# HGRN2 attention and a PReLU network on one core: the second layer by Strassen's seven products

## The chip, the core and the metric

The kernel runs on one NeuronCore of a Trainium2 chip. TensorE multiplies matrices into PSUM, VectorE and ScalarE work on tiles in SBUF and PSUM, GpSimd works on SBUF and issues transfers, and the sync engine issues transfers. The metric is the device time of one execution in microseconds, from the first to the last instruction on the core. Lower is better.

## What is computed

The first half is a gated linear recurrence over 768 time steps for 4 batches and 8 heads of dimension 48. Its output, rearranged to 3072 tokens of 384 numbers, goes through a two-layer network with a leaky activation whose slope is learned per column.

```python
f = 1 / (1 + exp(-f_logit))
for t in range(768):
    state = f[:, :, t, :, None] * state + einsum('bhd,bhe->bhde', k[:, :, t], v[:, :, t])
    y[:, :, t] = einsum('bhd,bhde->bhe', q[:, :, t], state)
x = y.transpose(0, 2, 1, 3).reshape(3072, 384)
h = x @ w_in                                     # 384 x 2048
g = maximum(h, 0) + alpha * minimum(h, 0)
out = g @ w_out                                  # 2048 x 384
```

All tensors are float32.

## The kernel before

Time is cut into chunks of C = 128, and a step handles one chunk of a pair of batches (U = 2), so a step has 256 tokens and there are 12 steps: `steps` runs over the six chunks, and within each over the two pairs. For each step there are four generators. Each does a piece of work up to a `yield`:

- `prepare` ("Q" for the step to come, "P" at the start) loads f, q, k, v, takes the sigmoid (L277), and builds the decayed forms of q and k on VectorE with some copies on ScalarE. It has six pieces. Lines L285 to L292 are in the first, the two scans L315 and L317 in the second, L319, L345 and the first L328 in the third, L366, L372 and further L328 in the fourth and fifth, the transpose L420 and the copies L415 in the sixth.
- `carry` ("O") has the matmuls `off` (L442) and `pd` (L482) and moves the recurrent state (`moved`, L492 and L496).
- `attend` ("S") has the matmuls `raw` (L518) and `qu` (L533) with masked copies on VectorE (L524, L539), the copies of `ad` into A on ScalarE (L561, eight of them in two pieces), the matmuls `py` (L572), and the copies and transfers that turn their result into xT, the network's input.
- `network` ("n") is the two-layer network of the step before.

The network has eight pieces for the first layer. Each multiplies two 128-column blocks of w_in with the 256 tokens of xT into one PSUM bank `ph` (L614); ScalarE takes relu(-h) (L620), and VectorE combines the two into the gate tile g (L623, two instructions). Four pieces for the second layer follow: the 16 row blocks of the gate against w_out, 128x384 a time, for the two batches of the step, 32 f32 matmuls in all (L639). Each f32 matmul is two records on TensorE in the profile. ScalarE copies the two results (L633), and the sync engine stores them. The gate is the stationary operand here and w_out is streamed.

PSUM has two pools: `psa`, two tiles of two banks that attention takes in turn, and `psn`, four single banks that `ph` and the second layer's results take in turn. A tile can be taken once the readers of the tile four takings earlier are done.

The order of the instructions on TensorE, VectorE and ScalarE is the order in which the generators are advanced. It is written out by hand as strings of letters, with a count where a piece is repeated: `first` has the strings of the opening rounds, `usual` that of all later ones. A generator that has no step left is passed over, so the last round has only "n".

```python
usual = "O n S n2 S n2 O n Q n Q2 n2 S3 n Q S n Q n Q"
```

At the start, the pieces "a", "w", "b", "v" bring w_in and w_out in: they are loaded as 64-bit words and turned to float32 with staging tiles, and the last part of w_out is added by transfers that GpSimd issues (L225).

Of the kernel before, what the change touches and what calls it, by code (L numbers as in the profile page):

```python
# [8 lines left out]
F32 = mybir.dt.float32  # L9
I16 = mybir.dt.int16  # L10
U16 = mybir.dt.uint16
BF16 = mybir.dt.bfloat16
# [3 lines left out]
ALU = mybir.AluOpType  # L16

C = 128
# [3 lines left out]
U = 2  # L22
# [3 lines left out]
WP = 768  # L26
AT_ONCE = 1
RAWS, TOPS, POWERS, LEADS = 4, 3, 1, 4
# [3 lines left out]
def kernel(  # L32
# [30 lines left out]
    nc = tc.nc  # L63
    B, NC, _, HP, _ = qT.shape
    DM = v.shape[-1]
    H = 2 * HP
    D = DM // H
    NF = alpha.shape[1]
    NK = DM // 128
    DF = NF * 128  # L70
    T = U * C
    W = U * HP * C
    GC = W // CH
    G = W // DB
    NJ = C // DB
# [11 lines left out]

    const = ctx.enter_context(tc.tile_pool(name="const", bufs=1))
    work = ctx.enter_context(tc.tile_pool(name="work", bufs=2))
    psa = ctx.enter_context(tc.tile_pool(name="psa", bufs=2, space=bass.MemoryType.PSUM))  # L90
    psn = ctx.enter_context(tc.tile_pool(name="psn", bufs=4, space=bass.MemoryType.PSUM))

# [3 lines left out]
    def bank(name):  # L96
        return psn.tile([128, 512], F32, tag="net", name=name)

    om = const.tile([128, NF], F32, tag="om", name="om")
    w_in_sb = const.tile([128, NK, DF], F32, tag="w_in", name="w_in_sb")  # L100
    w_out_sb = const.tile([128, NF, DM], F32, tag="w_out", name="w_out_sb")
    lvl = const.tile([128, 2, DB], F32, tag="lvl", name="lvl")
    nc.scalar.dma_start(out=lvl, in_=masks)
    nc.scalar.dma_start(out=om, in_=alpha)
# [58 lines left out]
    def load_weights(dst, src, name):  # L163

        rows_ = NK if dst is w_in_sb else 1
        pieces_ = dst.shape[1] * dst.shape[2] // WP
        if rows_ == 1:
            dst = dst.rearrange("p a n -> p (a n)").unsqueeze(1)
        width = WP // rows_
        words = src.rearrange("p (a n) -> p a n", a=rows_).bitcast(I16)  # L180
        at_once = AT_ONCE if rows_ > 1 else 0
        got = {}

        def of(n):
            return dst[:, :, n * width:(n + 1) * width]

        def by_row(t):
            return t.rearrange("p (a n) -> p a n", a=rows_)

        def upper(n):  # L190
            raw = work.tile([128, WP, 4], I16, tag="raw", name=f"{name}_raw{n}", bufs=RAWS)
            nc.sync.dma_start(out=raw.rearrange("p (a n) four -> p a (n four)", a=rows_)[:, :, 0:4 * width - 1],
                              in_=words[:, :, 4 * n * width + 1:4 * (n + 1) * width])

            top = raw[:, :, 2]
            pos = work.tile([128, WP], I16, tag="pos", name=f"{name}_pos{n}", bufs=TOPS)
            nc.scalar.activation(pos, top, AF.Relu, bias=bias[:, 0:1], scale=8.0)
            neg = work.tile([128, WP], I16, tag="wneg", name=f"{name}_neg{n}", bufs=TOPS)
            nc.scalar.activation(neg, top.bitcast(U16), AF.Relu, bias=bias[:, 1:2], scale=8.0)
            got[n] = raw, pos, neg  # L200

        def lead(n):
            raw, pos, neg = got[n]
            t = work.tile([128, WP], BF16, tag="lead", name=f"{name}_lead{n}", bufs=LEADS)
            nc.vector.tensor_tensor(t, pos.bitcast(BF16), neg.bitcast(BF16), ALU.subtract)
            got[n] = raw, t

        def power(n):
            raw, t = got[n]
            p = work.tile([128, WP], BF16, tag="power", name=f"{name}_power{n}", bufs=POWERS)  # L210
            nc.vector.tensor_scalar(p.bitcast(I16), t.bitcast(I16), -128, None, ALU.bitwise_and)
            got[n] = raw, t, p

        def rest(n):
            raw, t, p = got.pop(n)
            got[n] = t
            low = raw.bitcast(U32)[:, :, 0]
            nc.vector.scalar_tensor_tensor(of(n), by_row(low), 2.0 ** -36, by_row(p), ALU.mult, ALU.mult)

        def both(n):  # L220
            t = by_row(got.pop(n))
            if n < at_once:
                nc.vector.tensor_tensor(of(n), of(n), t, ALU.add)
            else:
                nc.gpsimd.dma_start(out=of(n), in_=t, accum_op=ALU.add)  # L225

        def uppers():
            for n in range(pieces_):
                upper(n)
                yield  # L230

        def rests():
            for n in range(pieces_ + 1):
                if n < pieces_:
                    lead(n)
                if n:
                    rest(n - 1)
                if n < pieces_:
                    power(n)
                if n:  # L240
                    both(n - 1)
                yield

        return uppers(), rests()
# [11 lines left out]
    def prepare(bp, c, x):  # L256
# [159 lines left out]
                               q3[rows(par)].rearrange("p (u h c) s t -> p u h c (s t)", h=HP, c=NC2)[:, :, :, cc, 0:CH])  # L416
        if c:

            kt = work.tile([128, 2 * WP], F32, tag="raw", name=f"kt_{i}", bufs=RAWS)
            nc.vector.transpose(kt[:, 0:W], ks.rearrange("p g s t -> p (g s t)"))  # L420
            ksn = x["ksn"] = work.tile([128, U, HP * 128], F32, tag="ksn", name=f"ksn_{i}", bufs=1)
            for a in range(4):
                n = min(32, D - 32 * (a % 2))
                for b in range(NJ):
                    nc.sync.dma_start(
                        out=ksn[32 * b:32 * (b + 1)].rearrange("p u (h x) -> p (u h) x", h=HP)[:, :, 32 * a:32 * a + n],
                        in_=kt[32 * a:32 * (a + 1), 0:W].rearrange("p (g b x) -> p g b x", b=NJ, x=32)[:, :, b, 0:n])
        yield

    def carry(bp, c, x):  # L430
# [175 lines left out]
    def network(bp, c, x):  # L606
        i = f"{bp}_{c}"
        xT = x["T"]
        gs = []
        for f in range(0, NF, 2):  # L610
            ph = bank(f"ph{f}_{i}")
            for kt in range(NK):
                for j in range(2):
                    nc.tensor.matmul(ph[:, j * T:(j + 1) * T], lhsT=w_in_sb[:, kt, (f + j) * 128:(f + j + 1) * 128],  # L614
                                     rhs=xT[:, kt], start=(kt == 0 and j == 0), stop=(kt == NK - 1 and j == 1),
                                     skip_group_check=True)

            neg = work.tile([128, 2, T], F32, tag="neg", name=f"neg{f}_{i}")
            phv = ph.rearrange("p (j t) -> p j t", j=2)
            nc.scalar.activation(neg, phv, AF.Relu, scale=-1.0)  # L620
            g = work.tile([128, 2, T], F32, tag="g", name=f"g{f}_{i}", bufs=8)
            for j in range(2):
                nc.vector.scalar_tensor_tensor(g[:, j], neg[:, j], om[:, f + j:f + j + 1], phv[:, j],  # L623
                                               ALU.mult, ALU.add)
            gs.append(g)
            yield

        po = [bank(f"po{u}_{i}") for u in range(U)]
        last = (bp, c) == steps[-1]

        def store(u):
            o = work.tile([128, DM], F32, tag="o", name=f"o{u}_{i}")
            nc.scalar.copy(o, po[u][:, 0:DM])  # L633
            t0 = ((U * bp + u) * NC + c) * C
            nc.sync.dma_start(out=out[t0:t0 + C], in_=o)

        for n, (f, u) in enumerate([(f, u) for u in range(U) for f in range(NF)] if last else
                                   [(f, u) for f in range(NF) for u in range(U)]):
            nc.tensor.matmul(po[u][:, 0:DM], lhsT=gs[f // 2][:, f % 2, u * C:(u + 1) * C], rhs=w_out_sb[:, f],  # L639
                             start=(f == 0), stop=(f == NF - 1))  # L640
            if last and (f, u) == (NF - 1, 0):
                store(0)
            if n % 8 == 7 and n != U * NF - 1:
                yield
        for u in range(1 if last else 0, U):
            store(u)
        yield

    steps = [(bp, c) for c in range(NC) for bp in range(B // U)]
    first = (
        "P2 a P w P a P a w O P w S a w S Q a O a w S2 Q w S Q S",
        "P a w a P w2 b n2 v O n b2 v S n v n P S b S v b n S v n b v Q b n b n v O v n v Q3 S2 n2 Q2",
        "O n2 S n2 S Q S2 n3 O n Q n Q2 n S2 n Q2 n",
        "n O n2 S n2 S Q n O Q n2 S Q n S n S Q2 S Q n2",
    )
    usual = "O n S n2 S n2 O n Q n Q2 n2 S3 n Q S n Q n Q"  # L660
    pieces = {key: part for keys, parts in (("aw", load_weights(w_in_sb, w_in, "w_in")),
                                            ("bv", load_weights(w_out_sb, w_out, "w_out")))
              for key, part in zip(keys, parts)}

    def begin(n):
        if n >= len(steps):
# [70 lines left out]
```

## Time and profile before

| | |
|---|---|
| time, median of 3 runs | 650.63 us (650.04 to 652.03) |
| span of the profiled execution | 649.8 us |
| TensorE matmuls (PE) busy | 608.4 us, 94% of the span |
| VectorE (DVE) busy | 423.8 us, 65% |
| ScalarE (ACT) busy | 255.0 us, 39% |
| GpSimd (POOL) busy | 67.7 us, 10% |
| first layer, L614 | 1152 records of 128x256 |
| second layer, L639 | 768 records of 128x384 |

PE means matmuls and PEld the loads of the stationary operand, which have their own row. A line such as `L639 PE MATMUL po<-w_out_sb,g 128*128 128x384 f32 x768` has the line in the kernel, the engine, what is written from what, the stationary shape, the moving shape and the number of instructions. In a wait such as `[1.01 <-ACT qd L280]`, the engine stood idle for 1.01 us before the instruction and ScalarE's instruction at line 280 ended that. An idle time matters only where it reaches the engine that sets the end.

### The profile page before, as it was taken

What the parts mean: (1) busy time and instruction counts of PE and PEld (TensorE: products, weight loads), DVE (VectorE), ACT (ScalarE), POOL (GpSimd) and SP (SyncE); (2) the same over time, 40 slices, a digit from 0 to 9 for tenths busy, and PEclk for the clock granted to TensorE, in tenths of its full rate; (3) what the DMA queues carried; (4) which work ended last, traced back from release to release, by engine and by line L of the source; (5) the groups of instructions that cost most, each with busy time, mean ns of one, the idle gap of its engine ahead of it and who ended that gap; (6) DMA issues with size and microseconds to landing.
All of it is one profiled execution on the core that took longest, in us unless ns stands there. A gap on an engine that the chain in (4) does not pass through costs nothing.

```text
span 649.8 us, 17589 instructions
## 1 busy us (share of the span) xinstructions
PE 608.4 (94%) x7580; PEld 451.3 (69%) x7580; DVE 423.8 (65%) x866; ACT 255.0 (39%) x466; POOL 67.7 (10%) x114
## 2 busy tenths in 40 slices
PE   0549799999999999999999999999999999999997
PEld 0447666866876876875875876876876786786874
DVE  6889788794595685686686687577577477450220
ACT  5676683432443161361360360461351351331210
POOL 9142221000000010000000000001001000000000
PEclk9998899999999999999999999999999999999999
DMA  7998985412223223313313313313313201101000
GB/s 256 274 251 224 270 223 133 100 47 61 45 80 74 73 56 72 72 41 86 73 35 90 74 34 90 75 34 90 65 44 88 49 30 35 42 1 25 24 1 24
DMA packets 73116, 56.22 MB, mean 87 GB/s; under 512 B 47408, under 2 KB 64944, under 8 KB 73040
## 3 DMA queue, kind: packets, MB, share of 16 engines
q0 software_dynamic: 10112, 27.53, 15.9%
q1 hardware_dynamic: 57536, 25.37, 15.6%
q10 hardware_dynamic: 5392, 2.21, 1.6%
q8 instruction: 60, 0.98, 0.6%
q14 instruction: 16, 0.13, 0.1%
HBM read 36.21 MB, written 4.72 MB: 63 GB/s over the span
## 4 chain that ended last, share of the span: by engine, by line
PE 91%; DVE 5%; issue 2%; ACT 1%; DMA 1%; DVEq 0%
PE ph L614 39%; PE po L639 38%; PE py L572 3%; PE raw L518 3%; PE qu L533 3%; PE pd L482 1%; PE off L442 1%; DMA f<-in_fT 1%; DVE ad L524 1%; PE pk L469 1%; DVE qd L285 0%; PE off L452 0%; DVE us L319 0%; DVE k L345 0%; ACT us L312 0%
## 5 line engine op out<-in xcount | busy, mean ns | idle before, releaser
L614 PE MATMUL ph<-xT,w_in_sb 128*128 128x256 f32 x1152 | 263.5, 386 | 3.9 <-issue 3.9
L639 PE MATMUL po<-w_out_sb,g 128*128 128x384 f32 x768 | 252.9, 488 | 0.0
L614 PEld LDWEIGHTS ph<-xT,w_in_sb 128*128 128x128 f32 x1152 | 217.6, 192 | 37.3 <-issue 7.5
L639 PEld LDWEIGHTS po<-w_out_sb,g 128*128 128x128 f32 x768 | 144.9, 190 | 96.8
L623 DVE SCALAR_TENSOR_TENSOR g<-neg,om,ph 128x256 f32<-128x256 f32 x192 | 83.2, 476 | 164.6 <-ACT neg L620 164.5
L620 ACT ACTIVATE neg<-ph 128x512 f32<-128x512 f32 x96 | 57.4, 600 | 169.1 <-PE ph L614 164.3
L633 ACT COPY o<-po 128x384 f32<-128x384 f32 x24 | 11.5, 478 | 145.5 <-PE po L639 145.5
L524 DVE COPY_PREDICATED ad<-mraw,raw 128x256 f32<-128x256 int32 (+1 forms) x96 | 42.3, 441 | 5.5 <-PE raw L518 3.0
L539 DVE COPY_PREDICATED ad<-mquad,qu 128x224 f32<-128x224 int32 (+6 forms) x140 | 41.9, 299 | 6.2
L561 ACT COPY A<-ad 32x256 f32<-32x256 f32 x96 | 38.4, 400 | 2.2 <-DVE ad L539 0.9
L328 DVE TENSOR_TENSOR us<-us,fs 128x768 f32<-128x768 f32 (+5 forms) x60 | 37.1, 618 | 0.3
L312 ACT COPY us<-qd 128x256 f32<-128x256 f32 x48 | 30.3, 668 | 9.9 <-DVE qd L285 9.8
L264 POOL DMA_DIRECT2D k<-in_kT x11 | 8.3, 759 | 233.7 <-PE raw L518 206.9
L285 DVE TENSOR_TENSOR qd<-qd,f 128x768 f32<-128x768 f32 (+2 forms) x36 | 27.1, 753 | 8.2 <-ACT qd L280 8.2
L572 PEld LDWEIGHTS py<-A,vs 128*64 128x64 f32 x768 | 25.0, 145 | 10.3 <-ACT A L561 8.1
L415 ACT COPY A<-q 48x512 f32<-48x512 f32 x44 | 27.1, 616 | 9.4 <-DVE f L410 4.5
L572 PE MATMUL py<-A,vs 128*64 128x64 f32 x768 | 26.9, 231 | 3.9 <-ACT A L561 3.9
L518 PE MATMUL raw<-qd,k 48*32 48x80 f32 x1536 | 23.7, 243 | 5.2 <-issue 3.9
L518 PEld LDWEIGHTS raw<-qd,k 48*32 48x32 f32 x1536 | 18.5, 109 | 13.6 <-issue 13.0
L442 PE MATMUL off<-q,kh 48*32 48x32 f32 x768 | 9.4, 199 | 18.4 <-DVE q L366 18.4
L581 ACT COPY y<-py 128x512 f32<-128x512 f32 x24 | 12.9, 589 | 34.2 <-PE py L572 34.1
L533 PE MATMUL qu<-us,k 48*32 48x112 f32 (+1 forms) x1536 | 25.7, 259 | 0.0
(85 smaller groups left out, 437.7 us busy)
## 6 DMA issues: line engine op xcount, KB each, us to landing
w_out_raw<-in_w_out SPq DMA_DIRECT2D x8, 767.8 KB, 6.4
w_in_raw<-in_w_in SPq DMA_DIRECT2D x8, 767.2 KB, 6.2
f<-in_fT POOLq DMA_DIRECT2D x11, 512.0 KB, 4.1
q<-in_qT POOLq DMA_DIRECT2D x11, 512.0 KB, 4.0
k<-in_kT POOLq DMA_DIRECT2D x11, 512.0 KB, 4.4
out<-o SPq DMA_DIRECT2D x24, 192.0 KB, 2.1
vs<-in_v POOLq DMA_DIRECT2D x22, 192.0 KB, 3.7
w_out_sb<-w_out_lead POOLq DMA_DIRECT2D x8, 384.0 KB, 6.3
```

The lines of the kernel that those rows point to most:

```text
L312: nc.scalar.copy(q4[:, :, :, r], qdv[r][:, :, :, 0])
L328: nc.vector.tensor_tensor(us[:, :, UO[m]:UO[m] + 4 * n].rearrange("p g (i r) -> p g i r", r=4), us[:, :, skip:skip + 4 * n].rearrange("p g ...
L518: nc.tensor.matmul(raw[DB * j:DB * (j + 1), par, hp * C:hp * C + QW], lhsT=k[r_, g * DB:(g + 1) * DB], rhs=qd[r_, g], start=True, stop=True)
L524: nc.vector.copy_predicated(adu[:, :, :, d:4], mraw[:, d, :, d:4].bitcast(I32).unsqueeze(1).broadcast_to((128, H, NB, n)), rv[:, :, QO[d]: ...
L533: nc.tensor.matmul(qu[DB * j:DB * (j + 1), par, hp * QS + 4:hp * QS + QL], lhsT=k4[r_, g * DB:(g + 1) * DB], rhs=us[r_, g, 4:QL], start=Tr ...
L539: nc.vector.copy_predicated(ad[:, u, :, :, 4 * m:DB], mquad[:, lo:lo + n].bitcast(I32).unsqueeze(1).unsqueeze(1).broadcast_to((128, 2, HP, ...
L561: nc.scalar.copy(A[s_, u, :, s_], ad[s_, u].rearrange("p r h t -> p (r h) t"))
L572: nc.tensor.matmul(py[64 * par:64 * par + 64, u, o:o + CH], lhsT=vs[bp][:, cc, u, hd * D:hd * D + 64], rhs=A[:, u, par * HP + hp, CH * cc: ...
L614: nc.tensor.matmul(ph[:, j * T:(j + 1) * T], lhsT=w_in_sb[:, kt, (f + j) * 128:(f + j + 1) * 128], rhs=xT[:, kt], start=(kt == 0 and j == ...
L620: nc.scalar.activation(neg, phv, AF.Relu, scale=-1.0)
L623: nc.vector.scalar_tensor_tensor(g[:, j], neg[:, j], om[:, f + j:f + j + 1], phv[:, j], ALU.mult, ALU.add)
L639: nc.tensor.matmul(po[u][:, 0:DM], lhsT=gs[f // 2][:, f % 2, u * C:(u + 1) * C], rhs=w_out_sb[:, f], start=(f == 0), stop=(f == NF - 1))
```

## The change

From the second step on, the second layer is computed as a product of 2 x 2 blocks. The tokens of the two batches are the two block rows of the gate, the two halves of the 2048 hidden columns its block columns, and w_out is cut into halves by rows and by columns. Winograd's form of Strassen's scheme needs seven products of half-size blocks (each eight matmuls of 128x192) where the plain form needs eight. In exchange it adds and subtracts blocks: four sums of gate blocks (S), four of w_out blocks (t1 to t4), and sums of the products.

- The gate becomes one tile that is kept for the whole kernel. In a changed step, the first layer's groups pair block f with block f + 8, so that both halves of the hidden columns come along together. After groups 4 and 8, VectorE makes the four gate sums for the four row blocks just finished (`sums`).
- The w_out sums are made once, on GpSimd, in the piece "W" (`halves_of_w_out`) of the second round, after the first step's network, which stays plain. t1 overwrites the block b12.
- The staging tiles of the weight loads move to a pool of their own, which is closed before the new tiles are allocated. The tile `kt` of L420, which shared a staging buffer, gets its own.
- Products one (a11 b11) and two (a22 t4) need no gate sum. Product one is copied by ScalarE (`kept`) and added on VectorE to product three; banks of products one and three go on accumulating products five and six. In all, six adds out of PSUM on VectorE and two copies on ScalarE replace the two copies of L633.
- The network has five pieces for the second layer in place of four, the last of them an add and a store alone; the order strings are extended, and in `usual` the third preparation piece moves behind the eighth first-layer group.

```diff
-        for f in range(0, NF, 2):
+        plain = (bp, c) == steps[0]
+        for f in range(NH):
             ph = bank(f"ph{f}_{i}")
+            tiles = (2 * f, 2 * f + 1) if plain else (f, f + NH)
...
-            g = work.tile([128, 2, T], F32, tag="g", name=f"g{f}_{i}", bufs=8)
-            for j in range(2):
-                nc.vector.scalar_tensor_tensor(g[:, j], neg[:, j], om[:, f + j:f + j + 1], phv[:, j],
+            for j, m in enumerate(tiles):
+                nc.vector.scalar_tensor_tensor(gate[:, m % NH, m // NH], neg[:, j], om[:, m:m + 1], phv[:, j],
                                                ALU.mult, ALU.add)
+            if not plain and f % 4 == 3:
+                sums(slice(f - 3, f + 1))
             yield
...
+        def product(to, of, by, more=False):
+            for f in range(NH):
+                nc.tensor.matmul(to[:, 0:DH], lhsT=of(f), rhs=by(f), start=(f == 0 and not more), stop=(f == NH - 1),
+                                 skip_group_check=True)
...
+        product(pa, a11, b11)
+        product(pb, a22, t4)
+        nc.scalar.copy(kept, pa[:, 0:DH])
+        yield
+        pc, pd = (bank(f"p{n}_{i}") for n in "cd")
+        product(pc, s2, t2)
+        product(pd, s1, t1)
+        nc.vector.tensor_tensor(u2, pc[:, 0:DH], kept, ALU.add)
+        yield
+        product(pa, a12, b21, more=True)
+        product(pc, s3, t3, more=True)
+        nc.vector.tensor_tensor(o0[:, DH:DM], pd[:, 0:DH], u2, ALU.add)
+        nc.scalar.copy(o0[:, 0:DH], pa[:, 0:DH])
+        yield
+        pe = bank(f"pe_{i}")
+        product(pe, s4, b22)
+        nc.vector.tensor_tensor(u3, pc[:, 0:DH], kept, ALU.add)
+        nc.vector.tensor_tensor(o1[:, 0:DH], pb[:, 0:DH], u3, ALU.add)
+        nc.vector.tensor_tensor(o1[:, DH:DM], pd[:, 0:DH], u3, ALU.add)
+        store(1, o1)
+        yield
+        nc.vector.tensor_tensor(o0[:, DH:DM], pe[:, 0:DH], o0[:, DH:DM], ALU.add)
+        store(0, o0)
+        yield
...
+        for to, x_, y_, op in ((s[:, 0, fs_], of(0, u1), of(1, u1), ALU.add),
+                               (s[:, 1, fs_], s[:, 0, fs_], of(0, u0), ALU.subtract),
+                               (s[:, 2, fs_], of(0, u0), of(0, u1), ALU.subtract),
+                               (s[:, 3, fs_], of(1, u0), s[:, 1, fs_], ALU.subtract)):
+            nc.vector.tensor_tensor(to, x_, y_, op)
...
+        for to, x_, y_ in ((late["t3"], b22, b12), (b12, b12, b11), (late["t2"], b22, b12), (late["t4"], b21, late["t2"])):
+            nc.gpsimd.tensor_tensor(to, x_, y_, ALU.subtract)
...
-    usual = "O n S n2 S n2 O n Q n Q2 n2 S3 n Q S n Q n Q"
+    usual = "O n S n2 S n2 O n Q n Q n Q n S3 n Q S n Q n Q n"
```

## Prediction

> **What bounds the kernel now.** I read the page first (busy shares, then the chain), then the chain in order of time for the period of a step, then the groups by shape for prices, then the timeline of one middle step, 308.6 to 358.1 us.
>
> ```profile
> PE 608.4 (94%) x7580; PEld 451.3 (69%) x7580; DVE 423.8 (65%) x866; ACT 255.0 (39%) x466; POOL 67.7 (10%) x114
> ...
> PE 91%; DVE 5%; issue 2%; ACT 1%; DMA 1%; DVEq 0%
> ```
>
> ```profile
> 358.09 2.79 PE ph L614 x12
> ...
> 384.02 5.16 PE po L639 x16
> 389.18 2.02 PE py L572 x64
> 391.20 15.68 PE po L639 x48
> 407.56 2.79 PE ph L614 x12
> ...
> 604.75 20.72 PE ph L614 x96
> 625.47 20.65 PE po L639 x64
> ```
>
> TensorE carries 91% of the chain. A middle step lasts 407.56 - 358.09 = 49.47 us, and inside it the first-layer (ph) and second-layer (po) matmuls and attention follow each other without a hole. One f32 matmul shows as two records. In the last step, which has nothing beside it, 96 ph records take 20.72 us, 216 ns each, and 64 po records 20.65 us, 323 ns each. So fewer TensorE columns shorten the run directly, as long as nothing makes TensorE wait. That is the whole question, so here is the stretch of a middle step from the sixth gate group on:
>
> ```profile
> 329.46 0.60 ACT L620 ACTIVATE neg<-ph 128x512 f32<-128x512 f32 x1 [3.06 <-PE ph L614]
> 330.08 1.06 ACT L277 ACTIVATE f<-f 128x1024 f32<-128x1024 f32 x1
> 331.74 1.06 ACT L280 COPY qd<-q 128x1024 f32<-128x1024 f32 x1
> 332.82 0.96 DVE L285 TENSOR_TENSOR qd<-qd,f 128x768 f32<-128x768 f32 x1 [1.01 <-ACT qd L280]
> 334.39 5.32 PE L639 MATMUL po<-w_out_sb,g 128*128 128x384 f32 x16
> 335.91 0.87 DVE L623 SCALAR_TENSOR_TENSOR g<-neg,om,ph 128x256 f32<-128x256 f32 x2
> 336.69 0.76 DVE L315 TENSOR_TENSOR_SCAN ps<-fs,ones 128x289 f32<-128x289 f32 x1
> 338.01 1.20 DVE L319 TENSOR_TENSOR us<-us,f 128x1024 f32<-128x1024 f32 x1
> 339.64 2.09 PE L572 MATMUL py<-A,vs 128*64 128x64 f32 x64
> 341.13 0.87 DVE L623 SCALAR_TENSOR_TENSOR g<-neg,om,ph 128x256 f32<-128x256 f32 x2
> ```
>
> The columns are start, length, engine, line. TensorE starts the second layer at 334.39. The seventh gate group is written by VectorE only at 335.91 and the eighth at 341.13, nearly 7 us after the second layer began. It costs nothing before the change, because po takes the gate tiles in rising order and needs the last two only in its last eighth. VectorE's lateness is thus hidden by the order of po, not by idle time.
>
> [...] the trace has 216 and 323, so I use it for 192 columns: 162.5 ns. [...] The trace's load records are longer (192 ns mean at L614), but they overlap:
>
> ```profile
> 339.64 1.95 PEld L572 LDWEIGHTS py<-A,vs 128*64 128x64 f32 x64 [0.55 <-ACT A L561]
> ```
>
> ```profile
> 59.13 1.08 PEld L469 LDWEIGHTS pk<-ident,ks 128*128 128x128 f32 x8
> ```
>
> 64 loads of mean 145 ns fit in 1.95 us, and eight 128-column loads (of transposes) in 1.08 us, so a record's length is not the spacing. I take 162.5; were it the record's 190, see the rivals. [...]
>
> **Part by part: TensorE.** Removed per step: 64 records of 323 ns, 20.65 us. Added: seven products of eight f32 matmuls, 112 records of 162.5 ns, 18.20 us. Gain 2.45 us in each of 11 steps, 27 us at most.
>
> **VectorE, ScalarE.** Eight sums of 512 columns: 684 ns by the 128x512 rows, about 0.6 start to start, four of them with a dependence 2.65 us. Six adds of 192 columns out of PSUM: the 48x384 add from pd takes 552 ns; 192 columns fewer at about 1 ns make 0.35. Together 7.4 us a step on VectorE, 34.5 to 42 of 49. ScalarE trades two copies of 478 ns for two of about 0.32.
>
> **A middle step, by the new order (n6 Q1 n7 Q2 n8 Q3 n9 S3 n10 Q4 S n11 Q5 n12 Q6 n13).** The first four sums stand behind gate 4 (ends 325.2) and push gate 5, the state update and gate 6 back 1.4 us or less; L285 waits for ScalarE's copy until 332.8 anyway, so this is absorbed, with 0.4 us to spare.
>
> Now the first product needs all of its gates f = 0..7 within one product: the eighth is read 14 records after its start, at 334.39 + 2.27 = 336.66. Gate 8 now stands before Q3 but still behind gate 7 and the scans, so it starts at 338.01 and its first half ends at 338.49. It is the stationary operand, so a load of 0.19 us comes before the matmul; with the semaphore TensorE goes on at about 338.75. **A new wait of 2.1 us per step**, with the remaining products and py queued behind it.
>
> Second, the copy "kept" stands before ScalarE's eight A copies (3.3 us) and can't start before product one ends, 339.3. The copies end at 343.0; py starts at 341.75, and its second half waits 0.2 to 0.3 us. Third, the sum of product three and kept on VectorE holds Q4, the state update and Q5 behind it until 346.9. These (0.35 + 3.7 + 2.15 + 0.35 + 3.2) and the first two result adds end at 357.4; those free the PSUM bank that the next step's first ph group takes at 357.8. No wait, by 0.4 us.
>
> TensorE ends the step's second layer at 334.39 + 2.6 + 2.1 + 2.6 + 2.3 (py with its wait) + 13.0 (five products) = 357.0, against 357.24. Gain 0.24 us per step for the seven steps with that order and a coming preparation: 1.7 us.
>
> **The other steps.** In the first changed step the sums delay gate 8 from 137.5 to 140.1, against a read at 139.0: 1.7 us of wait with the load. At its end the adds stand behind Q5 and Q6 and free the bank at 160.1, where the next ph began at 159.46: loss 0.7. In the second, gates 7 and 8 come behind the state update and scans (old 189.1, new 190.4), where the reads are due at 187.9: wait 3.75, loss 1.1 after the gain. The last but one has no preparation: gate 8 is in time, the A copies cost 0.3, gain 2.1. The last gains 2.5.
>
> **GpSimd, once.** Four subtractions of 1,536 elements: [...] The first changed product that reads them starts at about 141. [...] VectorE's work beside them between 111 and 125 reads one operand out of PSUM. I take 0.5 us, between 0 and 5 (a load held behind them).
>
> The store and the o tiles cost nothing: the last store is as large as before.
>
> **Sum.** 1.7 + 2.1 + 2.5 - 0.7 - 1.1 - 0.5 = 4.0 us; 650.6 - 4 = 646.6, and I write 647.
>
> **Rivals.**
> (a) The waits are hidden and the whole gain arrives: 650.6 - 27 = 624. For it: VectorE is at 65%. Against: the chain relu 6, sigmoid, copy, five products, gate 7, scans, gate 8 takes 9.4 us from the end of n6, and TensorE has 7.5 us of work until it needs gate 8. A half-way form, with the wait at 1 us, gives 7 x 1.1 more than forecast: 639.
> (b) Slower: 0.4 us of slack before the bank, and again before L285, is thin. If waits grow by 1 us in each of nine steps: 647 + 9 = 656. For it: VectorE goes to 85%, and each new wait stands in front of a queue. Against: both slacks come out positive.
> (c) Loads bind at the record's 190 ns: 112 x 27.5 ns = 3.1 us more per step, some hidden behind the gate wait: 647 + 11 x 2.5 = 675. The overlapping loads speak against it.
> (d) GpSimd's operations hold the loads of f, q, k of a coming step: up to 5 us once, 652: no change.
>
> **Chances.** Forecast 0.45, (a) with its half-way form 0.20, (b) 0.20, (c) 0.03, (d) 0.12. The range takes in the half-way form and (b): 636 to 657. Below 648.7 lie most of the forecast and (a): 0.57. Above 652.6 lie (b), (c) and a little of the rest: 0.26; between, 0.17.
>
> **What would show it.** Product records 162 ns apart, and a second layer of 18.2 us plus waits. A TensorE wait of about 2 us on the eighth gate in each middle step, under "waits" as the first product's line behind VectorE's gate; VectorE at 500 us busy; a middle period near 49.2 us; the last but one step some 2 us shorter. The forecast is wrong if gate 8 comes before 336.7 of this step, if records stand 190 ns apart, or if ph waits for a bank behind the result adds.

## The result, and the profile after

The changed kernel takes 658.56 us (median of 4 runs, 654.92 to 659.57) against 650.71. The ratio is 1.010, 95% interval 1.0063 to 1.0136: slower by about 1%. The forecast was 647 us, with a range up to 657. Every ratio below is to the kernel before as it ran beside that run, 650.7 to 652.7 us from session to session, so ratios compare more closely than times.

The page of the changed kernel, first the busy shares, then the shares by engine of the chain (the work that ended last, followed back from the end):

```profile
PE 590.5 (90%) x8108; PEld 522.2 (79%) x8108; DVE 512.0 (78%) x1020; ACT 251.4 (38%) x466; POOL 81.7 (12%) x118
...
PE 66%; DVE 22%; ACT 6%; issue 4%; DMA 2%; ACTq 0%; DVEq 0%
```

Matmul time fell by 18 us, yet the chain's TensorE share fell from 91% to 66%: VectorE now holds 22% of it. VectorE's busy time rose by 88 us. The chain in order of time shows where the loss is not, the middle rounds and the end:

```profile
275.19 2.79 PE ph L619 x12
...
310.26 2.80 PE pc L658 x16
313.06 2.60 PE pd L658 x16
...
324.14 2.79 PE ph L619 x12
...
615.11 20.72 PE ph L619 x96
635.83 2.60 PE pa L658 x16
...
651.43 2.61 PE pe L658 x16
```

A middle period is 324.14 - 275.19 = 48.95 us, 0.5 shorter than 49.47. A product takes 2.60 us for 16 records, 162.5 ns each. The last round's seven products, 635.83 to 654.04, take seven times that without a wait.

Start to start of the first ph group, read from each run's records, gives each round. A round has the number of the step whose network it holds, counted from one: round one (the second string of `first`) has the plain network of the first step and, at its end, the subtractions; round two is the first changed step; rounds four to ten have the string `usual` and a coming preparation.

| | before | changed |
|---|---|---|
| round two starts at | 110.9 us | 120.5 us |
| round two | 48.6 | 51.1 |
| round three | 50.1 | 54.7 |
| rounds four to ten, each | 49.5 | 48.9 |
| round eleven | 48.7 | 46.2 |

So 16.7 us are lost before round four starts, and rounds four to twelve give back about 9. Part of the 16.7 is not from the subtractions: round one already starts at 54.4 us here against 50.5 before, and between 51.8 and 55.1 in the other runs' profiles, so one pair of profiles is good to a few microseconds only. The end of round one and the start of round two, in the timeline:

```profile
102.83 3.44 POOL L714 TENSOR_TENSOR t<-w_out_sb 128x1536 f32<-128x1536 f32 x1 [0.82 <-DMA w_out_sb<-w_out_lead]
102.90 3.92 DVE L376 TENSOR_TENSOR kh<-k,ss 128x512 f32<-128x512 f32 x1
...
106.74 4.28 DVE L332 TENSOR_TENSOR us<-us,fs 128x640 f32<-128x640 f32 x1
106.89 3.44 POOL L714 TENSOR_TENSOR w_out_sb<-w_out_sb 128x1536 f32<-128x1536 f32 x1
...
118.63 0.68 DVE L370 TENSOR_TENSOR q<-us,ps 128x512 f32<-128x512 f32 x1
...
119.45 1.07 PE L446 MATMUL off<-q,kh 48*32 48x32 f32 x64 [8.07 <-DVE q L370]
```

L376 takes 3.92 us where it takes 0.68 elsewhere. It starts just after GpSimd's subtraction and ends 0.55 us after it, at 106.82; GpSimd's next subtraction starts at 106.89, and VectorE's next instruction ends after that one. The two take turns, one whole instruction each, four times: VectorE's four take 3.92, 4.28, 3.94 and 3.90 us, GpSimd's 3.44, 3.44, 3.44 and 3.75. L370, which off reads, starts 15.7 us after L376 where it took 2.55 us in the kernel before, so it is 13 us late, and TensorE idles 8.07 us. In this profile TensorE's clock is granted at half from 115.6, within that idle time, to 125.9 us.

### The profile page after: what moved, and what is told of

It reads as the page before. It is cut to its first block, busy times and chain, and to the rows that moved or that the text cites. A ratio compares the mean times of both kernels' runs of the same rounds, so it can differ in the third digit from the quotient of the medians.

```text
span 657.4 us, 18828 instructions
## 1 busy us (share of the span) xinstructions
PE 590.5 (90%) x8108; PEld 522.2 (79%) x8108; DVE 512.0 (78%) x1020; ACT 251.4 (38%) x466; POOL 81.7 (12%) x118
## 4 chain that ended last, share of the span: by engine, by line
PE 66%; DVE 22%; ACT 6%; issue 4%; DMA 2%; ACTq 0%; DVEq 0%
PE ph L619 28%; PE pc L658 8%; PE pa L658 5%; PE pb L658 5%; PE pe L658 4%; PE pd L658 4%; DVE gate L626 4%; DVE qd L289 3%; PE py L576 3%; PE raw L522 3%; PE qu L537 2%; DVE ad L543 2%; DVE ad L528 2%; DVE S L700 2%; ACT qd L284 1%
## 5 line engine op out<-in xcount | busy, mean ns | idle before, releaser
L626 DVE SCALAR_TENSOR_TENSOR gate<-neg,om,ph 128x256 f32<-128x256 f32 x192 | 82.9, 475 | 61.9 <-ACT neg L624 61.6
L658 PE MATMUL pa<-w_out_sb,gate 128*128 128x192 f32 x352 | 65.1, 332 | 14.0 <-DVE gate L626 14.0
L658 PEld LDWEIGHTS pa<-w_out_sb,gate 128*128 128x128 f32 x352 | 57.5, 190 | 19.3 <-DVE gate L626 18.6
L658 PE MATMUL pc<-t,S 128*128 128x192 f32 x352 | 61.6, 328 | 0.0
L658 PEld LDWEIGHTS pc<-t,S 128*128 128x128 f32 x352 | 57.4, 190 | 0.5
L332 DVE TENSOR_TENSOR us<-us,fs 128x768 f32<-128x768 f32 (+5 forms) x60 | 43.7, 728 | 0.1
L658 PE MATMUL pe<-w_out_sb,S 128*128 128x192 f32 x176 | 30.6, 327 | 1.6 <-DVE Csum L680 1.4
L658 PE MATMUL pb<-t,gate 128*128 128x192 f32 x176 | 32.1, 338 | 0.0
L446 PEld LDWEIGHTS off<-q,kh 48*32 48x32 f32 x768 | 8.4, 114 | 29.6 <-DVE q L370 18.5
```

Of the source, the lines that this page charges most:

```text
L332: nc.vector.tensor_tensor(us[:, :, UO[m]:UO[m] + 4 * n].rearrange("p g (i r) -> p g i r", r=4), us[:, :, skip:skip + 4 * n].rearrange("p g ...
L626: nc.vector.scalar_tensor_tensor(gate[:, m % NH, m // NH], neg[:, j], om[:, m:m + 1], phv[:, j], ALU.mult, ALU.add)
L658: nc.tensor.matmul(to[:, 0:DH], lhsT=of(f), rhs=by(f), start=(f == 0 and not more), stop=(f == NH - 1), skip_group_check=True)
```

## The experiments

The theory: a two-operand VectorE instruction waits for the whole GpSimd instruction in flight. The rival: the orders of the first changed rounds lose the time.

**Subtractions on VectorE.**

```diff
-            nc.gpsimd.tensor_tensor(to, x_, y_, ALU.subtract)
+            nc.vector.tensor_tensor(to, x_, y_, ALU.subtract)
```

> The four subtractions of w_out blocks run on VectorE, at the same place in its order; nothing else differs from the changed kernel. Theory (GpSimd's subtractions hold VectorE's two-operand instructions from 103 to 118 us, which makes TensorE idle 8 us [...]): VectorE needs 4 x 1.65 = 6.6 us for them instead of losing about 13, the 8 us idle time before the off matmuls goes, and the run takes 647 to 651 us. Rival (the loss before the fourth round comes from the new order of gates and products, not from GpSimd): within 2 us of the changed kernel, 656 to 660 us.

It took 654.25 us (649.71 to 656.27, 12 runs), ratio 1.0022 (0.9999 to 1.0045): better than the changed kernel, but by half of what was expected, and outside both ranges. Its profile is of the fastest run. There the wait before off is gone. VectorE needs 1.76 us for each subtraction, in front of its last preparation pieces; now qu waits 3.73 us behind them, and round two takes 54.2 us. Part of the price moved with the work.

**The same subtractions in the kernel before**, writing to an idle tile:

```diff
...
+        for x_, y_ in ((b22, b12), (b12, b11), (b22, b12), (b21, b22)):
+            nc.gpsimd.tensor_tensor(idle, x_, y_, ALU.subtract)
...
```

> The kernel before, plus four GpSimd subtractions of the same size on the same operands at the same place in GpSimd's order, written to a tile that nobody reads. Theory (they hold VectorE): each of four VectorE instructions after 103 us takes about 3.9 us instead of 0.7, TensorE idles before off, and the run takes 7 to 13 us longer than before, 658 to 664 us. Rival (GpSimd runs beside VectorE at little cost): 650 to 652 us, and VectorE's instructions keep 0.6 to 0.8 us.

It took 662.95 us, ratio 1.0166 (1.0132 to 1.0200): 11 us longer than the kernel before, from four instructions whose result nobody reads. Its timeline:

```profile
103.53 3.51 POOL L659 TENSOR_TENSOR idle<-w_out_sb 128x1536 f32<-128x1536 f32 x1 [0.73 <-DMA w_out_sb<-w_out_lead]
103.67 3.91 DVE L372 TENSOR_TENSOR kh<-k,ss 128x512 f32<-128x512 f32 x1
...
120.23 1.08 PE L442 MATMUL off<-q,kh 48*32 48x32 f32 x64 [8.04 <-DVE q L366]
```

This is the same picture without any of Strassen: 3.91 us for L372, 8.04 before off. The theory holds; GpSimd did not run beside VectorE at little cost.

**Gate 8 ahead of the scans** in the middle rounds:

```diff
-    usual = "O n S n2 S n2 O n Q n Q n Q n S3 n Q S n Q n Q n"
+    usual = "O n S n2 S n2 O n Q n2 Q2 n S3 Q n S n Q n Q n"
```

> The changed kernel with one order string different: in the middle rounds the eighth first-layer group stands before the scans, and the fourth preparation piece before the tenth network piece. Theory (the 1.9 us that product one waits for gate 8 are lost TensorE time in each of seven rounds): the gap before the last two records of product one shrinks from 1.5 us to below 0.8, the middle period goes from 48.9 to about 47.8 us, and the run takes 648 to 652 us. Rival (VectorE's queue sets the period, and the wait only moves to the next bank or to off): period and time as the changed kernel, 656 to 660 us.

It took 650.19 us (20 runs), ratio 0.9976 (0.9963 to 0.9989). The middle period is 47.6 to 47.8 us. From its first to its last record product one takes 3.10 us, 4.40 in the changed kernel and 2.44 where nothing hinders it. The rival, that the wait only moves, is out. The subtractions still cost their part: in its profile off does not wait, but qu waits 8.7 us in round two. There GpSimd was the first to wait: its first subtraction started at 101.65 us, 0.12 after a VectorE instruction, and lasted 6.86 us, while VectorE ran six such instructions, from 101.53 to 105.22, at their usual 0.55 to 0.82. The turns began after that. What decides which engine waits first is not shown.

**Subtractions in pieces** of 192 columns:

```diff
-            nc.gpsimd.tensor_tensor(to, x_, y_, ALU.subtract)
+            for f in range(NH):
+                nc.gpsimd.tensor_tensor(to[:, f], x_[:, f], y_[:, f], ALU.subtract)
```

> The changed kernel with each GpSimd subtraction cut into eight of 192 columns. If VectorE waits for the whole GpSimd instruction and the two then alternate, a VectorE instruction after 103 us takes about 1.1 us instead of 3.9, off waits 2 to 4 us instead of 8, the subtractions last some 30 us, and the run takes 650 to 655 us. If the two share bandwidth, VectorE is slowed as much as by the whole instructions: 656 to 660 us.

It took 648.95 us, ratio 0.9943 (0.9913 to 0.9973), a little below the range expected. The same work on the same engine, cut up, is worth 10 us:

```profile
103.30 7.84 POOL L715 TENSOR_TENSOR t<-w_out_sb 128x192 f32<-128x192 f32 x8 [0.82 <-DMA w_out_sb<-w_out_lead]
103.36 1.08 DVE L376 TENSOR_TENSOR kh<-k,ss 128x512 f32<-128x512 f32 x1
...
111.72 0.76 PE L446 MATMUL off<-q,kh 48*32 48x32 f32 x64
...
117.08 4.46 POOL L715 TENSOR_TENSOR t<-w_out_sb 128x192 f32<-128x192 f32 x8
...
120.48 1.66 DVE L626 SCALAR_TENSOR_TENSOR gate<-neg,om,ph 128x256 f32<-128x256 f32 x4 [0.95 <-ACT neg L624]
```

L376 takes 1.08 us, its 0.68 and one short wait. Off does not wait, where 2 to 4 us were expected; qu waits 1.18 us in round two. Eight pieces need 7.84 us beside such instructions. The eight from 117.08 need 4.46; VectorE was idle or did a transpose, a one-operand instruction, for much of that; the transpose kept its 1.25 us. The gate instructions at 120.48, with one operand in PSUM, keep their length with the last eight pieces running (121.48 to 125.94): four take 1.66 us, and 1.67 at 126.25, after the pieces.

**Pieces in the kernel before**: the edit of the pieces applied to the idle subtractions.

> The kernel before with the four idle GpSimd subtractions, each in eight pieces of 192 columns. Theory (a two-operand VectorE instruction waits for the one GpSimd instruction in flight, so the length of that instruction sets the loss): VectorE's instructions after 103 us take 1.1 us instead of 3.9, off waits under 1 us, and the run takes 651 to 655 us, against 663 with whole subtractions. Rival (the total GpSimd work counts): 658 to 664 us.

It took 656.02 us, ratio 1.0062 (1.0042 to 1.0081), 1 us over the range.

```profile
99.61 1.04 POOL L660 TENSOR_TENSOR idle<-w_out_sb 128x192 f32<-128x192 f32 x1
100.60 2.63 POOL L225 DMA_DIRECT2D w_out_sb<-w_out_lead  x3
...
105.09 8.01 PE L639 MATMUL po<-w_out_sb,g 128*128 128x384 f32 x24 [3.39 <-DMA w_out_sb<-w_out_lead]
...
106.60 1.07 DVE L366 TENSOR_TENSOR q<-us,ps 128x512 f32<-128x512 f32 x1
```

VectorE's instructions beside the pieces take 1.07 us, and off does not wait, so the theory's mechanism holds; but a loss came from elsewhere. In this build eight pieces, from 92.4 us to the one shown at 99.61, stand in GpSimd's queue ahead of three of the transfers that complete w_out, and po waits 3.39 us for one of them.

**No subtractions**: t2, t3, t4 filled with a constant, b12 left alone.

```diff
...
-            nc.gpsimd.tensor_tensor(to, x_, y_, ALU.subtract)
...
+            nc.gpsimd.memset(late[n], 0.03)
```

> The changed kernel without its four subtractions of w_out blocks: GpSimd fills t2, t3 and t4 with a constant, b12 stays as it is, so the second layer's values are not the product. Orders, products, sums and adds stay. Theory (the prediction missed by the GpSimd term alone, and its other terms hold): off waits less than 1 us in round two, the middle period stays 48.9 us, and the run takes 644 to 650 us. Rival (the orders of rounds two and three, which were under-estimated, make up much of the miss): 651 to 656 us.

It took 648.64 us, ratio 0.9944 (0.9923 to 0.9966). Off does not wait: at the start of round two the timeline has

```profile
103.92 0.69 DVE L376 TENSOR_TENSOR kh<-k,ss 128x512 f32<-128x512 f32 x1
104.06 4.00 POOL L713 MEMSET t<- 128x1536 f32 x3 [1.01 <-DMA w_out_sb<-w_out_lead]
...
112.36 0.76 PE L446 MATMUL off<-q,kh 48*32 48x32 f32 x64
```

Beside GpSimd's memsets the same VectorE instructions keep their length, L376 0.69 us. The subtractions account for 658.6 - 648.6 = 10 us, and the ratios give the same.

**Both mended, and the first rounds.** The next five combine the pieces with orders. First, pieces and gate 8 first:

> Both earlier edits at once: the subtractions in pieces of 192 columns and gate group 8 ahead of the scans in the middle rounds. If the two losses are separate, their gains add: 658.6 - 9.6 (pieces) - 8 (order) = 641, within 638 to 644 us, with middle periods of 47.6 to 47.8 us. If they are one loss seen twice, 647 to 650 us.

It took 638.70 us, ratio 0.9782 (0.9740 to 0.9824). The two gains add. Round three still takes 53.2 us. Then the middle string from round two on:

> As f2_pieces_gate8, and rounds two and three take the middle rounds' order string too. Theory (these two rounds lose because gates 7 and 8 stand behind the state update and the scans in their own strings, with waits of 1.5 to 1.9 us and a bank wait of 1.4 us): round three, 54.6 us in the changed kernel, falls to 48 to 51 us, and the run takes 635 to 639 us. Rival (round three is long because VectorE is late from round two, whatever its order): no shorter than f2_pieces_gate8, or longer because off stands first.

It took 637.86 us, ratio 0.9781 (0.9733 to 0.9828): not told apart from the run above. Round three falls to 47.8 us as the theory has it, but round two rises from 48.8 to 53.8, with waits of 1.3 us before qu and 2.5 before pd. The two rounds together take 101.6 us against 101.9, so the time moved from one to the other. In round two the middle string is worse than its own; whether round three is long by its own order or by what round two leaves behind, this run does not show. Then all three gates first:

```diff
-    usual = "O n S n2 S n2 O n Q n Q n Q n S3 n Q S n Q n Q n"
+    usual = "O n S n2 S n2 O n3 Q n S2 Q2 S n Q S n2 Q2 n"
...
```

> As f2_pieces_gate8, but in the middle rounds gates 6, 7 and 8 all stand ahead of the preparation, and the A copies ahead of its second piece; the two result adds stand ahead of its last two pieces. If the wait for gate 8 is the only one left, the middle period falls to the TensorE sum of about 47.0 us and the run to 636 to 640 us. If ScalarE's queue or the bank of the next round takes its place, the period stays at 47.6 us or more and the run at 641 us or more.

It took 641.76 us, ratio 0.9845 (0.9807 to 0.9884). Product one now takes its unhindered 2.44 us, but the period is 48.1 us: py waits 0.5 us for ScalarE's A copies and qu 0.3, so other waits took the gate's place. Then three plain steps, the subtractions moved to the turn of rounds three and four:

```diff
-        plain = (bp, c) == steps[0]
+        plain = (bp, c) in steps[:3]
...
```

> As f2_pieces_gate8, but the first three steps stay plain and most subtractions run at the turn from round three to four. Theory (rounds two and three lose by the waits of their changed steps): they take 48.5 to 50.2 us as in the kernel before, and the run takes 636 to 641 us, less what the subtractions cost in round four. Rival (the loss is that of the subtractions alone, and moves with them): the loss turns up in round four, and the run takes 641 to 648 us.

It took 635.35 us, ratio 0.9740 (0.9705 to 0.9775). Giving up Strassen in two more steps, with the subtractions moved out of the opening rounds, is a gain of some 3 us over pieces and gate 8 alone; which of the two edits makes it was not separated. Rounds two and three take 48.5 and 50.1 us as in the kernel before, round four 47.9. With two plain steps and the middle string from round three:

> As f4_three_plain_steps, but only the first two steps stay plain, and rounds from the third on take the middle order string. One more changed step gains up to 2.45 us, and round three, 50.1 us in its own string, falls to 47.6 to 49 us: 632 to 634 us. If VectorE is too late for off at the head of round three, the round keeps 50 us or more and the run takes 635 us or more.

It took 634.72 us, ratio 0.9713 (0.9677 to 0.9749), 0.7 us above the range's upper end and not told apart from three plain steps. Round three, changed and in the middle string, takes 48.8 us behind a plain round two, with 0.9 us of wait before qu. Both runs beat the kernel before by 2.6 to 2.9%, and by their ratios the changed kernel by 3.6 to 3.8%.

## Why the prediction was wrong

**The step that failed is "GpSimd, once".** It took 0.5 us, between 0 and 5, because the subtractions end long before their first reader, and because VectorE's work after 111 us reads PSUM. Their length no instruction of the kernel before had shown; they took 3.44 us each, the last 3.75. Two things were missed. The term asked who waits for the result, and not what the subtractions hold up while they run; and it looked at VectorE's operands only from 111 us on. The subtractions started at 103 us, and the kernel before, which is 1.1 us ahead at this point, shows what VectorE does from there:

```profile
101.78 0.68 DVE L372 TENSOR_TENSOR kh<-k,ss 128x512 f32<-128x512 f32 x1
102.39 0.81 DVE L328 TENSOR_TENSOR us<-us,fs 128x640 f32<-128x640 f32 x1
...
104.33 0.68 DVE L366 TENSOR_TENSOR q<-us,ps 128x512 f32<-128x512 f32 x1
...
110.22 0.76 PE L442 MATMUL off<-q,kh 48*32 48x32 f32 x64
```

This is the two-operand part of the preparation, with both operands in SBUF, and the q that off reads comes out of it. Each subtraction held one of these instructions for its whole length, L376 for 3.92 us in place of 0.68. That cost 10 us (no subtractions; pieces), or 11 when put alone into the kernel before. Rival (d), loads held behind GpSimd's operations, is not what cost the time: off waited for VectorE's q, not for a load.

**The other steps.** Without the subtractions the run takes 648.6 us, by its ratio 3.6 less than the kernel before; the working without its GpSimd term gives 4.5 less. That they lie so close is in part luck: the middle rounds gained more than forecast and round three lost more, and the two errors all but cancel.

- The product's price held: 162.5 ns a record, which is also the straight line through 216 ns at 256 columns and 323 at 384, so rival (c), loads at 190 ns each, is out.
- The wait for gate 8 in the middle rounds is there, forecast as 2.1 us. The timeline shows a hole of 1.49, but the ends of matmuls are modelled in the profile. By the starts of its records product one takes 4.40 us in place of 2.44, so the wait is 1.96:

```profile
255.52 0.86 DVE L626 SCALAR_TENSOR_TENSOR gate<-neg,om,ph 128x256 f32<-128x256 f32 x2
256.04 0.59 PE L658 MATMUL pa<-w_out_sb,gate 128*128 128x192 f32 x2 [1.49 <-DVE gate L626]
256.67 0.32 ACT L666 COPY Csum<-pa 128x192 f32<-128x192 f32 x1 [2.04 <-PE pa L658]
```

  The gain is 0.5 us a round against 0.24. ScalarE's copy is at the forecast 0.32 us. Gate 8 first in order took 1.2 us more off the period, so the wait was real lost time.
- Both slacks held: no middle round waits for the next ph bank. Rival (b), growing waits, is not what happened.
- Rounds two and three were forecast to lose 0.7 and 1.1 us. (The working's own figures for round three, a wait of 3.75 against a gain of 2.45, make 1.3.) Without the subtractions round two loses nothing (48.6 us) and round three 4.6. There product one takes 2.6 us too long, not 3.75. The term left out a wait of pe for a bank that the add L680 frees (1.39 us) and, in that profile, 3.4 us at half clock. With pieces and gate 8 first, round three has the same string, no half clock, and still loses 3.1 us; the waits named do not explain all of it.
- Round eleven gains 2.45 us, forecast 2.1, and round twelve 2.7, forecast 2.5.

Rival (a), the whole gain of 27 us, was not reached by any version: with the best middle order the period is 47.6 us, 1.9 of the possible 2.45 below 49.47. The rest is of the size of what product one still waits there, 3.10 us against 2.44. All three gates first took that wait away, and lost more elsewhere.

## What to carry to other kernels

Work put on an idle engine is not free because its result is needed late; ask also what it holds up while it runs, as L376 here, 3.92 us in place of 0.68, and place or cut it accordingly. When a matmul chain is cut into products, each product needs its last stationary block much sooner, so a producer that used to be late behind a rising order becomes a wait: move that producer ahead in its queue, but no further than the wait asks. Start such a scheme where the pipeline is steady; in the opening rounds here, leaving it out and moving the subtractions together were worth some 3 us.

## What was not expected of the hardware

- A VectorE instruction with two operands in SBUF that met a GpSimd subtraction waited until that whole instruction had ended, and the two engines then took turns: 0.68 us became 3.92 beside 3.44 us subtractions and 1.08 beside pieces of 192 columns. In the profile of gate 8 ahead of the scans GpSimd waited first, and its subtraction took 6.86 us. Beside GpSimd memsets the same instruction took 0.69, and four gate instructions with one operand in PSUM kept their 1.66 us beside the pieces.
- From within TensorE's idle time of 8 us on, the clock was granted at half for 10.2 us in the changed kernel and 6.8 in the kernel before with subtractions. This adds to the loss: off takes 1.07 us in place of 0.76 without subtractions. In the changed kernel 5.4 us of it lie in round two, which takes 51.1 us against 48.6 without subtractions, so by estimate the clock makes some 2.5 of the 10 us.
